# A new order for the first 330 of 1099 steps of a gated SSM-and-MLP kernel

## The chip, the cores and the metric

The kernel runs on one core of a Trainium2 chip. A core has five engines that each work through their own list of instructions: TensorE (PE, with its weight loads PEld), VectorE (DVE), ScalarE (ACT), GpSimd (POOL) and SyncE (SP), which here only issues DMAs. They meet at semaphores. The metric is the device time of one execution in microseconds.

## The reference

`S` is 2048, `D` 640, `F` 1536; all tensors are bfloat16. Two branches read the same `x` and are mixed by a gate per row.

```python
def _A_ref(q, k, v, shift_k, ssm_k, ssm_D):
    # k_shift: causal 4-tap filter of k along S, per column
    k_shift = sum(k_pad[:, t:t + S, :] * shift_k[:, ks - 1 - t] for t in range(ks))
    kv = k_shift * v
    # y: causal convolution of kv with ssm_k along S, by an FFT of length 2 S
    y = irfft(rfft(kv_pad) * rfft(ssm_k_pad))[:S] + kv * ssm_D
    return q * y

def _B_ref(x, w1, w2, w3, w4):
    h = _gelu(_layernorm(x) @ w1)
    # four column groups of h shifted by +1, -1, +2, -2 rows
    hs = concatenate([g0, g1, g2, g3]) @ w2
    x1 = x + hs
    return x1 + _gelu(_layernorm(x1) @ w3) @ w4

x = A_q
g = _sigmoid((x * gate_w).sum(-1, keepdims=True))
return g * _A_ref(x, A_k, ...) + (1 - g) * _B_ref(x, B_w1, ...)
```

(The sums and transforms are abridged here; `B_x` is not used.)

## The kernel before

Row `p * 16 + t` of a 2048 x 640 tensor lies in partition `p`, at place `t` of 16. Four places make a chunk, and there are four chunks, 0 to 3. The work is cut into 1099 numbered steps. The list `ORDER` names them in the order in which they are recorded; every engine gets its instructions in that order, and there is no scheduler behind it. A step `name.args:n` is the n-th part of a function, and letters such as `VAVA` in its name say which of its copies DVE (V) and ACT (A) make.

The first 330 steps hold, chunk by chunk:

- the loads of X (`load_x0` L193 in two halves for chunk 0, `load_x` L190), of k (`k_load:0` L563), of W1 in two halves (`load_w1` L197), of v in another row order by POOL's indirect DMA (`v_load` L173), and small ones (`load_cj` L542, `load_gw` L200, `d_fold:0` L401 and L402);
- row statistics (`x_stats`, DVE L685 to L695, ACT L679 and L681 for the rows given to it, the rstd on POOL L657 and L658) and the normalisation (`x_norm`, L662 on ACT, L664 on DVE);
- the transposition of the normalised chunk: for chunks 0 and 1 on PE (`x_turn`, L619, copied from PSUM at L360 by ACT or L362 by DVE), for chunks 2 and 3 by a DMA transpose that SP issues (L652);
- the W1 product (`mlp1:0`, five matmuls at L707 for each chunk and column group) and its GELU (`mlp1:1`, ACT L710);
- k's transposition on PE (L619 and L360 or L362 again), its wrap columns KW (`k_wrap`, L570 to L572), the tap diagonals DG (`kv_consts`, L552 and L553), and five `tap` steps, one for 128 columns each: 76 matmuls (L590) filter k, and DVE multiplies by v (L605 from PSUM, or L602 after an ACT copy at L599);
- the first transform stage (`step1`, pairs of matmuls at L423 and two copies each to a staging tile `stg`, stored to `S_x` by SP at L437 in two halves for each chunk);
- the loads of the filter (`load_h` L183 and L187) and its transposes on PE (`h_transpose` L390); the shifts of h on POOL (`h_shift` L742 to L761); the gate's rows and columns (`z_rows`, `z_cols`); the first W2 products (`w2`, L788, added to X by DVE at L791); sine tables by ACT (`f1_table`, `f4_table`, `t2_table`, L277).

Behind them come the rest of W2, the transform of the filter, the products and inverse transform, W3 (L840) and W4 (L867), and the output.

Two things tie the steps beside the order itself. PSUM has eight banks, handed out by the digits of `SLOTS["c"]` in the order of allocation. Tiles of one chunk (`kn`, `xn`, `stg` and others) share four row buffers, handed out by `SLOTS["row"]`; a tile that takes a buffer waits until the work on the one before it there has ended, a store included.

Of the kernel before, what the change touches and what calls it, by code (L numbers as in the profile page):

```python
# [41 lines left out]
def kernel(  # L42
# [24 lines left out]
        "c": "012345670124703510347205142356401723605162370514731057423671045261304732641374153670421350627413"  # L67
             "502634751264351270361427503164257364102546173045621537426107432715604371401362570164301257613045"
             "267236057416537621507362651374026372401534762501373150427102547535706432073125640736450750634127"
             "504763270415367204325170635147630125460327156034215760147362304167135620316425031672301402715320"  # L70
             "1724107361761423564023714053627501267420674256271306234",
        "row": "01230213021302320123012031203120310310303",
        "gt": "012301031010231012301201",
        "xt": "010101",
        "gq": "0120201201021020120122102121021021",
# [803 lines left out]
    def step4(t1, ev):  # L879
# [37 lines left out]
        "load_x0.1:0 "  # L917
        "consts0:1 "
        "warm:1 "
        "warm:2 "  # L920
        "pow0:0 "
        "kv_alloc:0 "
        "k_load.3.AVA:0 "
        "f4_table:0 "
        "x_stats.0.VVVA:0 "
        "warm:3 "
        "k_load.3.AVA:1 "
        "x_stats.0.VVVA:1 "
        "load_x.1:0 "
        "x_stats.0.VVVA:2 "  # L930
        "k_load.3.AVA:5 "
        "x_stats.0.VVVA:3 "
        "x_stats.0.VVVA:4 "
        "x_stats.0.VVVA:5 "
        "x_stats.0.VVVA:6 "
        "warm:4 "
        "row_order:0 "
        "k_load.2.VAV:0 "
        "f1_table:0 "
        "x_norm.0.VVAA:0 "  # L940
        "x_norm.0.VVAA:1 "
        "f4_table:1 "
        "x_stats.1.VVVV:0 "
        "k_load.3.AVA:2 "
        "load_x.3:0 "
        "x_norm.0.VVAA:2 "
        "x_stats.1.VVVV:1 "
        "k_load.3.AVA:3 "
        "x_turn.0.AAA:0 "
        "k_load.3.AVA:6 "  # L950
        "k_load.2.VAV:5 "
        "load_w1.1:0 "
        "x_norm.0.VVAA:3 "
        "k_load.2.VAV:1 "
        "x_stats.1.VVVV:2 "
        "x_turn.0.AAA:1 "
        "x_stats.1.VVVV:3 "
        "x_turn.0.AAA:2 "
        "x_stats.1.VVVV:4 "
        "load_w1.0:0 "  # L960
        "x_stats.1.VVVV:5 "
        "x_stats.3.VVAA:0 "
        "k_load.3.AVA:4 "
        "x_norm.1.VVVV:0 "
        "x_turn.0.AAA:4 "
        "k_load.2.VAV:3 "
        "x_turn.0.AAA:3 "
        "x_turn.0.AAA:5 "
        "x_stats.3.VVAA:1 "
        "x_norm.1.VVVV:1 "  # L970
        "x_norm.1.VVVV:2 "
        "v_load.2:0 "
        "k_load.0.AAV:0 "
        "f1_table:1 "
        "mlp1.0.2:0 "
        "mlp1.0.3:0 "
        "x_norm.1.VVVV:3 "
        "v_load.0:0 "
        "k_load.1.AVV:0 "
        "k_load.2.VAV:6 "  # L980
        "mlp1.0.0:0 "
        "load_x.2:0 "
        "x_stats.3.VVAA:2 "
        "x_turn.1.VVV:0 "
        "x_turn.1.VVV:4 "
        "mlp1.0.1:0 "
        "x_stats.3.VVAA:3 "
        "x_turn.1.VVV:1 "
        "k_load.2.VAV:4 "
        "x_stats.3.VVAA:4 "  # L990
        "x_stats.3.VVAA:5 "
        "k_load.0.AAV:3 "
        "x_turn.1.VVV:5 "
        "mlp1.0.3:1 "
        "x_stats.3.VVAA:6 "
        "x_turn.1.VVV:2 "
        "v_load.3:0 "
        "x_turn.1.VVV:3 "
        "k_load.1.AVV:3 "
        "w1_mixed:0 "  # L1000
        "v_load.1:0 "
        "mlp1.0.0:1 "
        "x_stats.2.VVAA:0 "
        "mlp1.0.2:1 "
        "k_load.0.AAV:1 "
        "mlp1.0.1:1 "
        "x_stats.3.VVAA:7 "
        "k_load.0.AAV:5 "
        "mlp1.1.2:0 "
        "x_norm.3.VVVV:0 "  # L1010
        "x_norm.3.VVVV:1 "
        "k_load.0.AAV:4 "
        "load_cj:0 "
        "k_load.0.AAV:2 "
        "mlp1.1.2:1 "
        "x_norm.3.VVVV:2 "
        "x_norm.3.VVVV:3 "
        "x_stats.2.VVAA:1 "
        "k_load.1.AVV:5 "
        "mlp1.0.4:0 "  # L1020
        "k_load.1.AVV:4 "
        "mlp1.0.4:1 "
        "k_load.1.AVV:1 "
        "d_fold:0 "
        "mlp1.1.4:0 "
        "x_turn.3.D:0 "
        "kv_consts:0 "
        "x_stats.2.VVAA:2 "
        "mlp1.1.0:0 "
        "k_load.2.VAV:2 "  # L1030
        "k_wrap:0 "
        "k_load.1.AVV:6 "
        "mlp1.1.4:1 "
        "k_load.0.AAV:6 "
        "x_stats.2.VVAA:3 "
        "t2_table:0 "
        "load_w2:0 "
        "mlp1.1.3:0 "
        "k_load.1.AVV:2 "
        "tap.3.VAVA:0 "  # L1040
        "mlp1.1.0:1 "
        "x_stats.2.VVAA:4 "
        "h_shift.1:0 "
        "mlp1.1.3:1 "
        "tap.4.VAAV:0 "
        "x_stats.2.VVAA:5 "
        "tap.3.VAVA:1 "
        "tap.3.VAVA:3 "
        "tap.3.VAVA:5 "
        "h_shift.0:0 "  # L1050
        "mlp1.1.1:0 "
        "tap.4.VAAV:7 "
        "x_stats.2.VVAA:6 "
        "tap.3.VAVA:4 "
        "tap.4.VAAV:1 "
        "load_h.2:0 "
        "tap.3.VAVA:7 "
        "z_cols:0 "
        "mlp1.1.1:1 "
        "load_gw:0 "  # L1060
        "tap.4.VAAV:5 "
        "tap.4.VAAV:3 "
        "mlp1.3.1:0 "
        "tap.3.VAVA:2 "
        "x_stats.2.VVAA:7 "
        "x_norm.2.AVVV:0 "
        "mlp1.3.1:1 "
        "mlp1.3.4:0 "
        "tap.4.VAAV:2 "
        "mlp1.3.0:0 "  # L1070
        "x_norm.2.AVVV:1 "
        "tap.4.VAAV:8 "
        "x_norm.2.AVVV:2 "
        "x_norm.2.AVVV:3 "
        "h_shift.0:1 "
        "tap.4.VAAV:6 "
        "tap.3.VAVA:6 "
        "mlp1.3.4:1 "
        "tap.4.VAAV:4 "
        "mlp1.3.0:1 "  # L1080
        "tap.2.AVAA:0 "
        "x_turn.2.D:0 "
        "h_shift.3:0 "
        "tap.0.AVAA:0 "
        "tap.2.AVAA:3 "
        "tap.2.AVAA:7 "
        "tap.2.AVAA:5 "
        "tap.3.VAVA:8 "
        "mlp1.3.3:0 "
        "tap.0.AVAA:3 "  # L1090
        "h_shift.0:2 "
        "tap.0.AVAA:5 "
        "tap.2.AVAA:8 "
        "h_shift.3:1 "
        "mlp1.3.2:0 "
        "tap.0.AVAA:4 "
        "tap.2.AVAA:6 "
        "tap.0.AVAA:1 "
        "mlp1.3.3:1 "
        "tap.0.AVAA:6 "  # L1100
        "tap.1.VAVA:0 "
        "tap.0.AVAA:7 "
        "tap.1.VAVA:5 "
        "tap.1.VAVA:1 "
        "tap.2.AVAA:4 "
        "mlp1.3.2:1 "
        "load_h.1:0 "
        "mlp1.2.2:0 "
        "tap.0.AVAA:8 "
        "tap.2.AVAA:1 "  # L1110
        "tap.1.VAVA:7 "
        "h_shift.1:1 "
        "tap.0.AVAA:2 "
        "load_h.3:0 "
        "mlp1.2.3:0 "
        "tap.1.VAVA:2 "
        "tap.1.VAVA:3 "
        "tap.2.AVAA:2 "
        "step1.KV.3.AAAVAVAAAV:9 "
        "tap.1.VAVA:8 "  # L1120
        "tap.1.VAVA:6 "
        "mlp1.2.2:1 "
        "mlp1.2.3:1 "
        "tap.1.VAVA:4 "
        "step1.KV.3.AAAVAVAAAV:11 "
        "step1.KV.3.AAAVAVAAAV:3 "
        "step1.KV.3.AAAVAVAAAV:10 "
        "step1.KV.3.AAAVAVAAAV:12 "
        "h_shift.0:3 "
        "step1.KV.3.AAAVAVAAAV:13 "  # L1130
        "step1.KV.3.AAAVAVAAAV:5 "
        "mlp1.2.4:0 "
        "step1.KV.3.AAAVAVAAAV:6 "
        "load_h.4:0 "
        "step1.KV.3.AAAVAVAAAV:0 "
        "step1.KV.3.AAAVAVAAAV:4 "
        "step1.KV.3.AAAVAVAAAV:14 "
        "h_shift.1:2 "
        "step1.KV.2.AVAVAVAAAA:6 "
        "z_rows:0 "  # L1140
        "z_rows:1 "
        "step1.KV.3.AAAVAVAAAV:2 "
        "step1.KV.3.AAAVAVAAAV:7 "
        "load_h.0:0 "
        "step1.KV.1.VAVAAAVVAA:0 "
        "step1.KV.3.AAAVAVAAAV:8 "
        "step1.KV.2.AVAVAVAAAA:8 "
        "step1.KV.3.AAAVAVAAAV:1 "
        "step1.KV.2.AVAVAVAAAA:3 "
        "z_rows:2 "  # L1150
        "mlp1.2.1:0 "
        "mlp1.2.1:1 "
        "h_shift.3:2 "
        "step1.KV.3.AAAVAVAAAV:16 "
        "step1.KV.1.VAVAAAVVAA:1 "
        "step1.KV.3.AAAVAVAAAV:15 "
        "mlp1.2.0:0 "
        "h_transpose.0.VV:2 "
        "step1.KV.2.AVAVAVAAAA:5 "
        "w2.0:0 "  # L1160
        "mlp1.2.4:1 "
# [903 lines left out]
```

## Time and profile before

| what | value |
|---|---|
| time, median of 3 runs | 231.19 us (227.55 to 232.08) |
| the profiled execution | 227.13 us, of which the span is 225.4 us |
| PE busy | 217.8 us, 97% of the span |
| DVE busy | 183.7 us, 81% |
| ACT busy | 171.4 us, 76% |
| granted TensorE clock | 1.0 |
| DMA moved | 57.61 MB |

The profile is one execution. A matmul's end is modelled, so a busy PE may still be slower than its best. In the timeline and the chain a row begins with its start and its length in us; a row of the timeline then has engine, line, operation, out<-in, the shape and the count, and in brackets how long the engine had sat idle and what ended that. In the chain each piece is what the next one waited for. In the table of waits the figures are the sum, the number of times and the longest.

### The profile page before, as it was taken

The page shows a single profiled execution, that of the slowest core. Times are in us where ns is not written, and L with a number is a line of the kernel's source. Part 1 is how long each engine was busy: PE and PEld are TensorE (multiplying, and loading weights), DVE is VectorE, ACT ScalarE, POOL GpSimd, SP SyncE. Part 2 cuts the span into 40 slices and gives each one's busy share as a digit, 9 for nine tenths or more (in the row PEclk, how much of TensorE's full clock was granted, in tenths as well). Part 3 has the DMA queues.
Part 4 walks back from the last instruction along what each step waited for, and adds up shares of the span by engine and source line. Part 5 has one row for each costly group of instructions (what it writes and reads, how often), then busy time and mean ns, then how long its engine had stood idle before and what let it go on. Part 6 is the DMA issues. An engine that isn't in the chain of part 4 may idle for free.

```text
span 225.4 us, 6053 instructions
## 1 busy us (share of the span) xinstructions
PE 217.8 (97%) x2427; PEld 121.5 (54%) x2428; DVE 183.7 (81%) x447; ACT 171.4 (76%) x341; POOL 38.1 (17%) x91
## 2 busy tenths in 40 slices
PE   8989999899999999999999999999999999999994
PEld 2557455447846563345664444556533547657762
DVE  7898998868889969963899988989999841439994
ACT  4899988787999999999987597967988450266450
POOL 4247246816000431300600000000000000000000
PEclk9999999999999999999999999999999999999999
DMA  6999998892998999999989570690794879429914
GB/s 226 374 376 344 258 280 170 317 364 107 361 365 355 348 295 265 410 334 343 254 219 338 116 243 0 191 379 17 119 305 166 249 259 366 175 60 305 324 70 179
DMA packets 41770, 57.61 MB, mean 256 GB/s; under 512 B 18446, under 2 KB 34446, under 8 KB 41486
## 3 DMA queue, kind: packets, MB, share of 16 engines
q1 hardware_dynamic: 41166, 54.60, 75.4%
q0 software_dynamic: 576, 2.62, 3.1%
q8 instruction: 19, 0.31, 0.6%
q14 instruction: 9, 0.07, 0.1%
HBM read 34.93 MB, written 18.35 MB: 236 GB/s over the span
## 4 chain that ended last, share of the span: by engine, by line
PE 79%; DMA 9%; DVE 4%; ACT 4%; issue 1%; POOL 1%; SPq 0%; ACTq 0%
PE ps L840 24%; PE ps L867 23%; PE psw L788 7%; PE ps L465 5%; PE ps L893 4%; DMA X<-in_A_q_dram 4%; PE psm L707 4%; DMA xt<-xn 3%; PE psz L228 3%; PE ps L512 3%; PE ps L423 2%; PE pst L390 2%; DVE X L791 2%; ACT stg L360 2%; DMA S_x<-stg 2%; PE psk L590 1%
## 5 line engine op out<-in xcount | busy, mean ns | idle before, releaser
L840 PE MATMUL ps<-x1t,W 128*128 128x512 bf16 x240 | 56.1, 380 | 0.1
L867 PE MATMUL ps<-W,gt 128*128 128x320 bf16 (+2 forms) x383 | 55.1, 299 | 0.1
L867 PEld LDWEIGHTS <-gt 128*128 128x128 bf16 x384 | 36.2, 98 | 17.7 <-issue 3.0
L844 ACT ACTIVATE gt<-ps 128x512 bf16<-128x512 f32 x48 | 27.6, 609 | 19.0 <-PE ps L867 10.6
L840 PEld LDWEIGHTS <-W 128*128 128x128 bf16 x240 | 21.9, 98 | 28.7 <-issue 5.9
L360 ACT CAST stg<-ps 128x512 bf16<-128x512 f32 x55 | 28.6, 604 | 2.3 <-PE ps L423 2.0
L870 DVE SCALAR_TENSOR_TENSOR X<-ps,OMG,X 128x320 bf16<-128x320 f32 (+2 forms) x32 | 17.2, 547 | 11.9 <-PE ps L867 11.7
L707 PE MATMUL psm<-xt,WA 128*128 128x512 bf16 x100 | 23.4, 379 | 1.9 <-DMA WA<-in_B_w_dram 0.8
L360 ACT CAST gs<-ps 128x320 bf16<-128x320 f32 x41 | 15.6, 440 | 8.8 <-PE ps L512 4.8
L788 PE MATMUL psw<-WA,HT 128*128 128x320 bf16 x116 | 21.4, 300 | 0.0
L362 DVE CAST XS<-ps 128x512 bf16<-128x512 f32 x19 | 12.5, 684 | 6.7 <-PE ps L465 6.7
L362 DVE CAST stg<-ps 128x512 bf16<-128x512 f32 x25 | 15.8, 683 | 1.9 <-PE ps L423 1.9
L707 PEld LDWEIGHTS <-WA 128*128 128x128 bf16 x100 | 9.2, 97 | 12.9 <-DMA WA<-in_B_w_dram 1.0
L360 ACT CAST hs<-ps 128x512 bf16<-128x512 f32 x28 | 15.0, 605 | 1.4 <-PE ps L465 1.4
L791 DVE SCALAR_TENSOR_TENSOR X<-psw,X 128x320 bf16<-128x320 f32 x32 | 14.5, 487 | 1.6 <-PE psw L788 1.6
L897 ACT ACTIVATE y<-ps,GS 128x320 bf16<-128x320 f32 x22 | 10.4, 526 | 5.7 <-PE ps L893 3.5
L710 ACT ACTIVATE HT<-psm 128x512 bf16<-128x512 f32 x20 | 11.8, 617 | 3.6 <-PE psm L707 3.5
L788 PEld LDWEIGHTS <-HT 128*128 128x128 bf16 x116 | 10.7, 98 | 6.8 <-issue 3.1
L362 DVE CAST gs<-ps 128x320 bf16<-128x320 f32 x23 | 10.7, 484 | 2.4 <-PE ps L512 1.7
L797 ACT ACTIVATE jk<-X 128x640 bf16<-128x640 bf16 x16 | 12.2, 761 | 0.5 <-DVE X L791 0.4
L788 PE MATMUL psw<-WA,HM 128*128 128x320 bf16 x44 | 12.3, 299 | 0.0
L360 ACT CAST XS<-ps 128x512 bf16<-128x512 f32 x21 | 11.8, 607 | 0.5 <-PE ps L465 0.3
(151 smaller groups left out, 346.6 us busy)
## 6 DMA issues: line engine op xcount, KB each, us to landing
S_x<-stg SPq DMA_DIRECT2D x8, 640.0 KB, 4.3
S_h<-stg SPq DMA_DIRECT2D x8, 640.0 KB, 4.8
ax<-S_x SPq DMA_DIRECT2D x8, 640.0 KB, 5.9
ax<-S_h SPq DMA_DIRECT2D x8, 640.0 KB, 8.1
S_g<-gs SPq DMA_DIRECT2D x8, 640.0 KB, 3.6
W<-in_B_w_dram SPq DMA_DIRECT2D x2, 1920.0 KB, 9.1
kn<-in_A_k_dram SPq DMA_DIRECT2D x4, 640.0 KB, 6.9
E<-in_A_ssm_k_dram SPq DMA_DIRECT2D x5, 512.0 KB, 6.1
```

Source lines behind the costliest of these rows:

```text
L360: A.copy(out=dst, in_=src)
L362: V.tensor_copy(out=dst, in_=src)
L465: PE.matmul(ps[j][q:q + 32, lo - 512 * u:hi - 512 * u], lhsT=CMP[HALF[j], 8 * b + 4 * h + i, c, :], rhs=st[name, 2 * b + h][HALF[j], i, lo ...
L707: PE.matmul(ps[:].rearrange("p (a b) -> p a b", a=4), lhsT=W1N[:, k, 160 * u:160 * u + P] if u < 4 else W1M[:, k, :], rhs=xt[:, :, k, :], ...
L710: A.activation(out=st["HT"][:, 4 * c:4 * c + 4, u, :], in_=ps[:].rearrange("p (t b) -> p t b", t=4), func=ACT.Gelu_apprx_tanh)
L788: PE.matmul(ps[:], lhsT=h_tile(f, t1), rhs=W2P[:, f, o:o + W], start=(f == 0), stop=(f == 4))
L791: V.scalar_tensor_tensor(out=X1[:, t1, o:o + W], in0=box["ps"][:], scalar=1.0, in1=X[:, t1, o:o + W], op0=ALU.mult, op1=ALU.add, accum_out ...
L797: A.activation(out=jk[:], in_=X1[:, t1, :], func=ACT.Square, accum_out=S12[:, 1, t1:t1 + 1])
L840: PE.matmul(ps[:].rearrange("p (a b) -> p a b", a=4), lhsT=st["W3"][:, k, f * P:(f + 1) * P], rhs=xt[:, :, k, :], start=(k == 0), stop=(k ...
L844: A.activation(out=st["gt", c, f // 4][:, f % 4, :], in_=ps[:], func=ACT.Gelu_apprx_tanh)
L867: PE.matmul(ps[:], lhsT=st["gt", c, f // 4][:, f % 4, i * P:(i + 1) * P], rhs=st["W4"][:, f, o:o + w], start=(f == 0), stop=(f == FC - 1))
L870: V.scalar_tensor_tensor(out=X1[:, t1, o:o + w], in0=box["ps"][:], scalar=OMG[:, t1:t1 + 1], in1=X1[:, t1, o:o + w], op0=ALU.mult, op1=ALU ...
```

## The change

The first 330 entries of `ORDER` are put in another sequence, and the letters of 21 of their functions change, so that some copies move between DVE and ACT. The last 769 entries are the same. `SLOTS` is renumbered to fit. No function changes, and every instruction that was there is there, but for one load of ACT's function tables, which the new order does not need.

```diff
-        "row": "01230213021302320123012031203120310310303",
+        "row": "01230120132030201320132103210321031031010",
...
-        "open.L1.left:0 "
-        "open.A2.right:0 "
-        "consts0:0 "
-        "load_x0.0:0 "
-        "warm:0 "
...
+        "open.L1.left:0 open.A2.right:0 warm:0 warm:1 warm:2 warm:3 warm:4 load_x0.0:0 consts0:0 consts0:1 "
```

On SP, at the program's start, the loads stood like this before (X is `A_q`, kn a chunk of k, WA with `B_w` first W1 and further down W2, E the filter, cr the taps, dr ssm_D, GW the gate weights):

```order
L193 DMA X<-in_A_q_dram 128x1280 x2
L563 DMA kn<-in_A_k_dram 128x2560
L190 DMA X<-in_A_q_dram 128x2560
L563 DMA kn<-in_A_k_dram 128x2560
L190 DMA X<-in_A_q_dram 128x2560
L197 DMA WA<-in_B_w_dram 128x5x320 x2
L563 DMA kn<-in_A_k_dram 128x2560 x2
L190 DMA X<-in_A_q_dram 128x2560
L542 DMA cr<-in_A_shift_k_dram 128x5x4
L401 DMA dr<-in_A_ssm_D_dram 1x3x128
L402 DMA dr<-in_A_ssm_D_dram 1x2x128
L652 DMA_TRANSPOSE xt_504<-xn 128x20x128
```

and now:

```order
L193 DMA X<-in_A_q_dram 128x1280 x2
L190 DMA X<-in_A_q_dram 128x2560
L563 DMA kn<-in_A_k_dram 128x2560
L190 DMA X<-in_A_q_dram 128x2560
L563 DMA kn<-in_A_k_dram 128x2560
L197 DMA WA<-in_B_w_dram 128x5x320 x2
L563 DMA kn<-in_A_k_dram 128x2560 x2
L542 DMA cr<-in_A_shift_k_dram 128x5x4
L200 DMA GW<-in_gate_w_dram 128x5x1
L190 DMA X<-in_A_q_dram 128x2560
L652 DMA_TRANSPOSE xt_777<-xn 128x20x128
L183 DMA E<-in_A_ssm_k_dram 128x2048
```

X and k have changed places among the first four chunk loads: X came in the chunk order 1, 3, 2 behind chunk 0 and comes as 3, 1, 2; k came as 3, 2, 0, 1 and comes as 2, 3, 1, 0. The last chunk of X stands behind the taps and the gate weights. The transpose shown is that of chunk 3.

On DVE, ahead of that transpose, this stood before (b and the L686 rows are statistics, the last L664 row is the normalisation of chunk 3, xt the transposed chunk 1):

```order
L362 COPY xt<-pst 128x1024
L203 COPY WA<-WA 128x640
L685 BN_STATS b_433<-X 128x6 x2
L686 BN_AGGR mv<-b_433 128x2
L664 TENSOR_SCALAR xn<-X,RS,NB 128x640 x4
L362 COPY KT<-pst 128x1024
L552 TENSOR_REDUCE i_507<-IDB 128x32
L553 TENSOR_TENSOR DG<-i_507,cr 128x640
```

and now, where the first L664 row is chunk 1 and the second chunk 3:

```order
L664 TENSOR_SCALAR xn<-X,RS,NB 128x640 x4
L570 MEMSET KW 128x15
L571 COPY KW<-KT 128x15x64
L572 COPY KW<-KT 128x15x63
L362 COPY KT<-pst 128x1024 x2
L552 TENSOR_REDUCE i_460<-IDB 128x32
L553 TENSOR_TENSOR DG<-i_460,cr 128x640
L362 COPY xt<-pst 128x1024
L362 COPY xt<-pst 128x512
L664 TENSOR_SCALAR xn<-X,RS,NB 128x640 x4
L685 BN_STATS b_660<-X 128x6 x2
L686 BN_AGGR mv<-b_660 128x2
```

The wrap columns and the diagonals have moved ahead of chunk 3's normalisation, and chunk 2's statistics behind it.

On ACT, around the copy of the gate rows (zr), the new order is this, where HT is a GELU of `mlp1`, the two stg rows ahead of zr belong to chunk 1 of the first transform and the stg rows behind it to chunk 2:

```order
L360 CAST stg<-ps_1136 128x512
L360 CAST stg<-ps_1130 128x512
L723 COPY zr<-psz 128x512
L360 CAST stg<-ps_1181 128x512
L710 ACTIVATE HT<-psm_1189 128x4x128
L360 CAST stg<-ps_1185 128x512
L360 CAST stg<-ps_1179 128x512
L710 ACTIVATE HT<-psm_1210 128x4x128
```

Chunk 1 now goes through the first transform together with chunk 3, ahead of chunk 2; before, chunks 1 and 2 both followed chunk 3, mixed with each other. By `SLOTS["row"]` the row behind zr takes the buffer of chunk 3's upper half, and the second stg row behind it that of chunk 1's upper half.

More of the change, by code (lines that the diff above doesn't have):

```diff
@@ L933 @@
[L933 to L990, printed above, removed]
@@ L1011 @@
[L1011 to L1072, printed above, removed]
@@ L1073 @@
[L1073 to L1132, printed above, removed]
@@ L1269 @@
-        "step1.HT0.2.VAVAAAAAAA:6 "
-        "load_w3:0 "
-        "w2.6:0 "
-        "step1.HT0.2.VAVAAAAAAA:2 "
-        "i_tables:1 "
-        "step1.HT0.2.VAVAAAAAAA:7 "
-        "w2.10:0 "
-        "w2.2:2 "
-        "w2.5:1 "
-        "step1.HT0.2.VAVAAAAAAA:11 "
-        "d_fold:1 "
-        "step1.HT0.2.VAVAAAAAAA:8 "
-        "w2.8:0 "
-        "step1.KV.0.VAAVAAAAAV:15 "
-        "w2.1:4 "
-        "w2.6:1 "
-        "w2.8:1 "
-        "w2.12:0 "
-        "step1.HT0.2.VAVAAAAAAA:10 "
@@ L1560 @@
-        "x1_norm.2.AVVV:5 "
-        "w3.1.2:1 "
-        "product.1:3 "
-        "product.1:4 "
-        "product.6:0 "
-        "step3.7.AAAAAVAV:6 "
-        "w4.0:3 "
-        "w3.1.9:1 "
-        "step2.h.0.AAVAAAAAVA:4 "
-        "step3.7.AAAAAVAV:9 "
-        "gather.h.2:0 "
-        "step3.7.AAAAAVAV:7 "
-        "product.6:1 "
-        "w3.1.1:0 "
-        "step3.1.VAAVVVAA:5 "
-        "step3.1.VAAVVVAA:7 "
-        "x1_norm.3.AVAA:1 "
-        "w3.1.8:0 "
-        "x1_norm.3.AVAA:2 "
@@ L2008 @@
-        "store.8:1 "
-        "close.L2:0 "
-        "close.C:0 "
[169 rows of a table added]
     ).split()
```

887 lines of the change are left out of this document (7 added, 880 removed), and 168 rows, old and new, of the table ORDER.

## The prediction

> **What bounds the kernel now.** I read the page's busy shares first, then busy time by stretch, then the chain of waits, then the timeline of the first 60 us.
>
> ```profile
> PE 217.8 (97%) x2427; PEld 121.5 (54%) x2428; DVE 183.7 (81%) x447; ACT 171.4 (76%) x341; POOL 38.1 (17%) x91
> ```
>
> In the table by stretch, the columns are the stretch, its length, busy us of PE, PEld, DVE, ACT and POOL, the clock, the DMA share and GB/s.
>
> ```profile
> 32.00:65.10 33.10, 32.24 (x467) 19.51 (x467) 27.42 (x63) 28.42 (x51) 14.85 (x34) 1.00 0.81 274
> 65.10:88.90 23.80, 23.66 (x165) 13.04 (x162) 21.04 (x75) 22.44 (x48) 4.81 (x11) 1.00 1.01 327
> 88.90:225.40 136.50, 133.02 (x1454) 72.35 (x1454) 106.41 (x201) 93.57 (x196) 5.90 (x18) 1.00 0.71 226
> ```
>
> From 65.1 us on PE is full. The 3.5 us that it lacks in the last row lie nearly all behind its last matmuls, which end at 221.3 by the chain:
>
> ```profile
> 219.00 2.34 PE ps L867 x10
> ```
>
> The 769 steps that stay as they are begin, on PE, with the third pair in this row of PE's timeline (64.65, 64.88, 65.09):
>
> ```profile
> 64.65 0.82 PE L423 MATMUL ps<-KV,F 64*128 64x512 bf16 x6
> ```
>
> So the change is worth what it moves that moment, 65.09 us: behind it nothing can take up a delay and nothing can lose a gain. The reordered part, by the chain:
>
> ```profile
> 8.96 1.01 ACT KT L360
> 9.97 0.82 ACT xn L662
> ...
> 12.09 0.91 ACT xt L360
> ...
> 13.42 8.33 DMA X<-in_A_q_dram
> ...
> 21.78 0.90 DVE b L685 x2
> ...
> 23.14 1.15 DVE xn L664 x3
> ...
> 24.32 7.63 DMA xt<-xn
> ...
> 32.00 3.41 PE psm L707 x15
> 35.41 2.00 PE psk L590 x151
> ...
> 40.83 0.59 ACT yk L599
> ...
> 44.31 3.59 ACT stg L360 x7
> ...
> 47.91 4.30 DMA S_x<-stg
> ```
>
> Chunk 2 of X lands at 21.75; the statistics of chunk 2 stand in DVE's order ahead of the normalisation of chunk 3; that ends at 24.3, its DMA transpose lands at 31.95, and PE starts the W1 products of chunk 3 at 32.00. PE's own waits up to 65.1 us are few; the four largest (sum, times, longest):
>
> ```profile
> PE psz L228 <- DVE NPI L248: 1.0, 1, 1.0
> PE psm L707 <- DMA WA<-in_B_w_dram: 0.8, 1, 0.8
> PE psm L707 <- ACT yk L599: 0.8, 1, 0.8
> PE pst L619 <- DMA kn<-in_A_k_dram: 0.7, 1, 0.7
> ```
>
> They sum to 3.3 us. The first is the start itself, so an order without any wait would save little over 2.3 us, or 1.0%.
>
> **The start.** The transfers land by their place in SP's queue: the third at 8.3, the fourth at 9.85, the fifth at 11.4, W1 at 14.2.
>
> ```profile
> 4.36 0.74 ACT L679 ACTIVATE jk<-X 128x640 bf16<-128x640 bf16 x1 [2.36 <-DMA X<-in_A_q_dram]
> 5.22 0.74 ACT L681 ACTIVATE jk<-X 128x640 bf16<-128x640 bf16 x1
> 6.07 1.28 ACT L277 ACT_TABLE_LOAD   x1
> 7.14 0.16 DVE L695 TENSOR_SCALAR VE<-mv 128x3 f32<-128x3 f32 x1
> 8.29 0.86 PE L619 MATMUL pst<-IDB,kn 128*128 128x128 bf16 x12
> 9.85 0.89 DVE L685 BATCH_NORM_STATS2 b<-X 128x6 f32<-128x320 bf16 x2 [0.32 <-DMA X<-in_A_q_dram]
> 11.43 0.86 PE L619 MATMUL pst<-IDB,kn 128*128 128x128 bf16 x12 [0.71 <-DMA kn<-in_A_k_dram]
> 14.22 3.41 PE L707 MATMUL psm<-xt,WA 128*128 128x512 bf16 x15 [0.82 <-DMA WA<-in_B_w_dram]
> ```
>
> W1 keeps its place, sixth and seventh, in both orders; "ahead of two k chunks" was so before, and I cost it at nothing. The third is now chunk 3 of X. ACT takes three statistics passes of it before it normalises chunk 0, at 0.86 each (4.36 to 5.22): 8.3 + 2.6 = 10.9. Then come two normalisations (0.82), one k copy (1.01 with its latency, 0.9 at pace), and the small and the large copy of the transposed chunk 0 (0.5 and 0.9): 10.9 + 1.6 + 0.9 + 1.4 = 14.8. The W1 products start there instead of at 14.2, 0.6 late. The table load at 6.07 is gone, since the order needs four loads and not five; ACT waited for data there anyway (2.36 idle), so it is worth nothing. F4's table leaves DVE's start, whose time goes into waiting for X. On the PE the five warm-up steps now run in one piece; they end before the fourth transfer at 9.85, which holds the first k chunk.
>
> **DVE up to chunk 3's transpose.** Here lies the term that counts. The normalisation of chunk 3 no longer waits for chunk 2 of X; behind it go 0.9 of chunk 2's statistics (21.78 row) and 0.9 of F4's small operations. But ahead of it now stand the wrap columns KW and the diagonals DG, and copies of k trade places with ACT:
>
> ```profile
> 24.82 0.36 DVE L552 TENSOR_REDUCE i<-IDB 128x32 bf16<-128x128 bf16 x1
> 25.21 0.83 DVE L553 TENSOR_TENSOR DG<-i,cr 128x640 bf16<-128x640 bf16 x1
> 25.95 0.68 DVE L362 COPY KT<-pst 128x1024 bf16<-128x1024 bf16 x1
> 26.57 0.41 DVE L571 COPY KW<-KT 128x960 bf16<-128x960 bf16 x1
> 26.89 0.80 DVE L572 COPY KW<-KT 128x945 bf16<-128x945 bf16 x1
> ```
>
> DG is 1.2, KW 1.1 (26.57 to 27.69), two k copies 1.2 at a pace of 0.6: 3.5 in. Going out are the 1.8 named and two small shares that went to ACT (0.4). Net +1.3. Idle time grows too: about 1.2 until chunk 3 lands at 8.3 (the statistics of chunk 0, which end at 7.3 today, end near 7.0 without F4) and 0.4 until the fifth transfer, against the 0.8 that DVE waits for X today: with 0.2 for ACT's late last sum, +0.7 to +1.0. I take +1.95 in all: the transpose is issued at 24.3 + 1.95 = 26.25. It lands 6.6 to 7.6 us later if it behaves as the two in this stage did; I take their median (the last figure of a row):
>
> ```profile
> 19.85 0.94 POOL L173 DMA_INDIRECT KV<-in_A_v_dram,ROWS  x1 [0.30 <-issue]
> ...
> KV<-in_A_v_dram,ROWS POOLq DMA_INDIRECT x4, 7.8
> x1t<-xn SPq DMA_TRANSPOSE x4, 5.1
> xt<-xn SPq DMA_TRANSPOSE x2, 7.1
> ```
>
> 26.25 + 7.1 = 33.35. What PE does before chunk 3 is the same amount as today: nine W1 steps and three tap steps in place of ten and two (1.1 against 1.0 each, the 32.00 and 35.41 rows), so without waits it would be ready at about 32.1. It waits 1.25, and starts chunk 3 at 33.35 instead of 32.00: **+1.35**. Today's 0.8 wait for the yk copy comes from a W1 product right behind the last tap step, which now has copies before it: **-0.75**.
>
> Queues passed: on SP the gate weights and cr now stand ahead of chunk 2 of X, which DVE reaches only at 26.3, so it has time. On POOL the last v chunk, issued at 19.85 today, moves behind chunk 3's rstd, 1.3 later; with 7.8 to land it is there at 28.9, and DVE's first tap product, which waits for all four, is due at 28.6: 0.3 that only DVE pays. d_fold's loads and the gate columns move to places where PE and DVE have other work; the columns cost the same matmuls wherever they are.
>
> **The stores.** A chunk of the first transform needs two of four row buffers. Chunks 3 and 1 now take all four, so the first ACT copy and the first DVE copy of chunk 2 wait for the store of chunk 3's upper half. From 33.35, PE has eight W1 steps (8.8), two tap steps (2.0) and seven pairs (1.7) until chunk 3 is through, and ACT three copies (0.5 each): stored at 47.4, landed 4.3 later at 51.7. ACT stands there from 49.4: it waits 2.3, and behind it queue the GELU of the next W1 products and the copies that free PE's banks. DVE waits 0.6, and later about 1.6 for chunk 2's own store, before it empties chunk 0. PE has eight banks to fill meanwhile. The cost for PE is between 0 and those 2.3 + 1.6. Today's like wait (47.91 to 52.21) cost PE almost nothing, as this row shows, so I take **+0.3**.
>
> ```profile
> 50.00:55.00 5.00, 4.90 (x48) 3.62 (x46) 3.79 (x9) 4.79 (x11) 3.59 (x6) 1.00 0.20 80
> ```
>
> Sum: 1.35 - 0.75 + 0.3 = +0.9 us. The profiled execution took 227.13 us (225.4 of span and 1.7 around it), so it would be 228.0.
>
> **The rivals.** *The transpose is quick.* The later four took 5.1, not 7.1: landed at 31.35, no wait on PE, and then 32.1 - 32.0 - 0.75, about -0.65: 226.5. For it: with the four X and k loads over by then, less lies beside it. Against it: the v chunk and W2 still do. The Trainium skill's "DMA: Bandwidth & Descriptors", section "Latency and other measured facts", gives a DMA transpose 261 GB/s or more; 655 KB would then be an estimated 2.5 us, landing at 28.8. The 7.1 row is far under that rate, so the trace so far disagrees; by that rule too PE would not wait, and the time is the same 226.5, from the rows as above.
>
> *The stores bind.* ACT's 2.3 and DVE's 1.6 fall on PE whole, because the eight banks hold nothing but results those two have yet to copy: 1.35 - 0.75 + 3.9 = +4.5, 231.6. It decides at the second pair of chunk 2: if a bank for it comes free only after 51.7, PE stands. Against it: two of the steps in between need banks that DVE frees.
>
> *It nets out.* The waits change places and the moment 65.09 does not move: 227.1. It lies inside my own sum's error, and I count it with the forecast.
>
> **How the numbers follow.** The forecast, +0.9 with 0 to +2.5 around it, 54%; the quick transpose 24%, and 5% more by the skill's rule; the stores 14%; 3% for what I do not see. The four executions known took 227.13, 227.55, 231.19 and 232.08 us: they differ by more than any term here, and the shown median, 231.19, is 1.8% over the profiled one. I put the 0.9 on the middle of the four, (227.55 + 231.19) / 2 = 229.4: 230.3. The range goes from 227.13 - 1.3 = 225.8 (a quick transpose with a little more, on a fast execution) to 232.1 + 1.5 = 233.6; the stores on a fast execution, 231.6, are inside. Two per cent, 4.6 us, is about what this kernel's measurement can tell from no change. A gain of that size would need more than all of PE's waits; I leave 6% for it. The stores reach it at their full price only: with what I do not see, 11% for slower. 83% for no difference.
>
> **What would show it.** Right: the first W1 product of chunk 3 near 33.3 with PE waiting for the transpose, the first at 14.8, the third tail pair near 66, and PE full from there on. The DVE step is wrong if the transpose is issued before 25.5; the landing is wrong if it takes under 6 us; the stores are wrong if PE shows waits for ACT or DVE copies between 49 and 61 of over 1 us. The whole is wrong if PE, behind 66 us, shows waits that it does not have today.

## The result, and the profile after

The changed kernel takes 228.96 us (median of 20 runs), the kernel before 227.67 (median of 20). The ratio is 1.0058, with a 95% interval of 1.0037 to 1.0078: slower by 0.6%, 1.3 us. A second timing of the same pair gave 1.0067 (1.0030 to 1.0105). The median of 231.19 shown before the change came from three runs, two of them long ones.

The page's first part of the kernel after, and its busy time by stretch (the stretch, its length, busy us of PE, PEld, DVE, ACT and POOL, the clock, the DMA share, GB/s), cut at the places that answer to those of before:

```profile
PE 218.4 (96%) x2428; PEld 121.4 (53%) x2428; DVE 184.3 (81%) x448; ACT 169.5 (74%) x336; POOL 38.0 (17%) x91
```

```profile
33.16:66.53 33.37, 32.59 (x405) 18.81 (x396) 29.73 (x85) 26.91 (x48) 15.72 (x34) 1.00 0.86 286
66.53:88.57 22.04, 21.65 (x157) 12.41 (x154) 19.25 (x68) 20.52 (x44) 4.18 (x8) 1.00 1.02 306
88.57:227.90 139.33, 134.91 (x1464) 72.88 (x1463) 108.37 (x208) 95.51 (x199) 6.53 (x21) 1.00 0.72 227
```

The kept 769 steps begin on PE with the third pair of this row of its timeline, at 66.52. (Ten of these 769 names carry the changed letters; behind the tail pair DVE and ACT still have the same instructions in both kernels.)

```profile
66.08 0.82 PE L423 MATMUL ps<-KV,F 64*128 64x512 bf16 x6
```

One trace each would mislead here, so I took two more of both kernels. The third tail pair stands at 65.09, 64.73 and 64.66 in the kernel before and at 66.52, 65.30 and 66.44 in the kernel after. The means, 64.83 and 66.09, differ by 1.26 us, close to the 1.3 that the times show, though the three traces of the kernel after lie 1.2 us apart. The start makes most of that spread. PE's first W1 product comes at 14.22, 13.81 and 13.79 in the kernel before and at 14.82, 13.38 and 14.54 in the kernel after, and from there to the tail pair it is 50.9 us in all three traces of the one and 51.7, 51.9 and 51.9 in those of the other. So 0.95 of the 1.26 lies behind the start and is there in every trace; 0.3 lies in the start, and that part is uncertain. PE's waits up to there (sum, times, longest), kernel after, first trace:

```profile
PE psk L590 <- DVE KV L605: 1.1, 3, 0.4
PE pst L619 <- DMA kn<-in_A_k_dram: 1.1, 2, 0.9
PE psz L228 <- DVE NPI L248: 1.0, 1, 1.0
PE psm L707 <- DMA xt<-xn: 0.5, 1, 0.5
PE pst L619 <- ACT xn L662: 0.3, 1, 0.3
PE psm L707 <- ACT xt L360: 0.2, 1, 0.2
```

The first row is new, and in all three traces (1.1, 1.1, 1.0); the row for k is in two of them. The new one is at the tap step ahead of chunk 3. This is PE's timeline there, and under it DVE's and POOL's:

```profile
28.11 2.33 PE L707 MATMUL psm<-xt,WA 128*128 128x512 bf16 x10
30.37 0.23 PE L590 MATMUL psk<-DG,KT 32*128 32x128 bf16 x1
30.97 0.21 PE L590 MATMUL psk<-DG,KT 32*128 32x128 bf16 x1 [0.37 <-DVE KV L605]
31.57 0.21 PE L590 MATMUL psk<-DG,KT 32*128 32x128 bf16 x1 [0.39 <-DVE KV L605]
32.16 0.38 PE L590 MATMUL psk<-DG,KT 32*128 32x128 bf16 x13 [0.39 <-DVE KV L605]
...
33.16 3.41 PE L707 MATMUL psm<-xt,WA 128*128 128x512 bf16 x15
```

```profile
27.68 0.21 DVE L686 BATCH_NORM_AGGREGATE mv<-b 128x2 f32<-128x12 f32 x1
30.22 2.49 DVE L605 TENSOR_TENSOR KV<-psk,KV 128x512 bf16<-128x512 f32 x4 [2.33 <-DMA KV<-in_A_v_dram,ROWS]
```

```profile
16.88 1.01 POOL L657 TENSOR_TENSOR RS<-VE,EXPO 128x4 f32<-128x4 f32 x1 [7.83 <-DVE VE L695]
...
18.34 1.22 POOL L173 DMA_INDIRECT KV<-in_A_v_dram,ROWS  x1 [0.18 <-issue]
...
23.67 1.02 POOL L173 DMA_INDIRECT KV<-in_A_v_dram,ROWS  x1 [0.16 <-issue]
```

Read from the bottom: POOL idles 7.83 us until chunk 1's statistics are done, and all four gathers of v stand behind that rstd. The first is issued at 18.34, where it was 15.84 before; the packets of the last one end at 29.30. DVE is ready for its first tap product at 27.9 and stands 2.33 us for that gather (2.1 to 2.3 in the three traces). Four products that read PSUM (L605) come at once then, and PE's third tap step, which needs the four banks that they free, takes 30.37 to 33.16: 2.8 us instead of 1.1 (2.8 and 2.6 in the other two traces). The order before reaches its first tap product three us after its last gather's packets have ended (27.66):

```profile
30.98 0.42 DVE L602 TENSOR_TENSOR KV<-yk,KV 128x512 bf16<-128x512 bf16 x1
```

The loss goes on behind chunk 3's first products. The next two tap steps take 2.4 to 2.5 us in the three traces of the kernel after and 1.9 to 2.0 in those of the kernel before; in the middle of them PE pauses for 0.2 to 0.3 us, for nothing that the view names:

```profile
37.51 0.75 PE L590 MATMUL psk<-DG,KT 32*128 32x128 bf16 x45 [0.23 <-issue]
```

Against these losses stand two waits of the kernel before: one of 0.2 to 0.5 for a GELU, which is gone, and one of 0.8 to 1.1 ahead of chunk 2's products, of which 0.4 to 0.8 is left.

Chunk 3's transpose was issued at 25.89 and landed 6.7 later, at 32.6, half a us ahead of the product that needs it. Nothing waited for it.

Behind the tail pair the first two traces seemed to say more: PE ends 156.9 us after it in the kernel before and 158.0 in the kernel after, with two waits that were not there before (kernel after, PE, from 66 us on):

```profile
PE ps L867 <- DMA W<-in_B_w_dram: 1.0, 1, 1.0
PE psw L788 <- ACT stg L360: 0.4, 1, 0.4
```

The third trace of the kernel *before* shows the same two:

```profile
PE ps L867 <- DMA W<-in_B_w_dram: 0.9, 1, 0.9
PE psw L788 <- ACT stg L360: 0.4, 1, 0.4
```

They come with a slower first transpose of X1 on SP (start, length of its issue), here in the kernel before, first and third trace:

```profile
78.09 4.40 SPq L821 DMA_TRANSPOSE x1t<-xn  x1
```

```profile
77.66 5.69 SPq L821 DMA_TRANSPOSE x1t<-xn  x1
```

So they do not need the new order. Whether it makes them more frequent stays open: that transpose pauses, by 0.15 to 1.95 us, in all eight traces of the new order and its variants, and in three of the six of the old order and its variants. In the six traces of the two kernels themselves PE ends 2.2 us later on the mean, 1.26 of it at the tail pair and 0.9 behind. The times, 1.3 us and 1.5 in the second timing, have room for only a part of that 0.9.

### The profile page after: what moved, and what is told of

Its sections match the earlier page's. It is cut to its first block, busy times and chain, and to the rows that moved or that the text cites. A ratio compares the mean times of both kernels' runs of the same rounds, so it can differ in the third digit from the quotient of the medians.

```text
span 227.9 us, 6050 instructions
## 1 busy us (share of the span) xinstructions
PE 218.4 (96%) x2428; PEld 121.4 (53%) x2428; DVE 184.3 (81%) x448; ACT 169.5 (74%) x336; POOL 38.0 (17%) x91
## 4 chain that ended last, share of the span: by engine, by line
PE 73%; DMA 14%; DVE 6%; POOL 3%; issue 1%; SPq 1%; DVEq 0%; POOLq 0%
PE ps L867 23%; PE ps L840 20%; PE psw L788 8%; DMA W<-in_B_w_dram 5%; PE psm L707 4%; DMA X<-in_A_q_dram 4%; PE ps L893 4%; PE ps L465 4%; PE ps L423 4%; PE ps L512 3%; DMA KV<-in_A_v_dram,ROWS 3%; DMA xt<-xn 3%; PE pst L390 2%; DVE b L685 1%; POOL KV L173 1%; DVE X L791 1%
## 5 line engine op out<-in xcount | busy, mean ns | idle before, releaser
L360 ACT CAST stg<-ps 128x512 bf16<-128x512 f32 x51 | 27.1, 600 | 5.1 <-DMA S_x<-stg 2.0
L707 PE MATMUL psm<-xt,WA 128*128 128x512 bf16 x100 | 23.8, 380 | 0.8 <-DMA xt<-xn 0.5
L362 DVE CAST stg<-ps 128x512 bf16<-128x512 f32 x29 | 18.4, 683 | 2.7 <-DMA S_x<-stg 1.6
L707 PEld LDWEIGHTS <-WA 128*128 128x128 bf16 x100 | 8.9, 97 | 11.9 <-issue 2.0
```

The lines of the kernel that those rows point to most:

```text
L360: A.copy(out=dst, in_=src)
L362: V.tensor_copy(out=dst, in_=src)
L707: PE.matmul(ps[:].rearrange("p (a b) -> p a b", a=4), lhsT=W1N[:, k, 160 * u:160 * u + P] if u < 4 else W1M[:, k, :], rhs=xt[:, :, k, :], ...
```

## The experiments

All of them compute the whole reference. An experiment is the named kernel with rows of `ORDER` moved; `SLOTS` stays as it was, except in the last one. Ratios are to the kernel before.

### The last gather ahead of the rstd

```diff
+"v_load.3:0 "
 "x_stats.3.VVAA:7 "
...
-"v_load.3:0 "
```

> The kernel after, with one row moved on POOL: the gather of the last v chunk (v_load.3) stands ahead of chunk 3's rstd again, as it did before the change. In the kernel after, it is issued at 23.67, lands at 30.1, and DVE waits 2.3 us for it ahead of its first tap product; the third tap step on PE (30.37) then takes 2.86 us instead of 1.1. The prediction's step (the gather is late because it was put behind that rstd, which takes 1.3 on POOL): it lands 1.3 earlier, at about 28.8, the third tap step loses some 1.3 us less, and the first chunk-3 W1 product is left to its transpose, which goes from 32.6 to about 33.5, because the rstd that the normalisation needs is now 1.0 later. Rival (the four gathers move one after the other, from 20.3 to 29.3, about 2.2 us each, so that the place of the last one's issue does not matter as long as it is ahead of 26.6): it lands at 29.8 to 30.1 as now, DVE waits as now, chunk 3 starts at 33.2 to 33.5, and the third tail pair stands at 66.5 to 67.0; time against the kernel after +0.0 to +0.4 us.

Measured: 1.0078 (1.0049 to 1.0108), no better than the kernel after. The gather did come earlier, its packets ending at 27.60 against 28.22 to 29.30. But the 1.0 to 1.3 us of the rstd that it passed went to the other side, as DVE's waits show:

```profile
DVE xn L664 <- POOL NB L658: 0.7, 1, 0.7
DVE KV L605 <- DMA KV<-in_A_v_dram,ROWS: 0.5, 1, 0.5
```

DVE now waits for chunk 3's rstd and reaches the taps later. PE's third tap step did shrink, to 1.7 us (29.46 to 31.16), but PE lost that elsewhere: it waits 1.1 us for chunk 2's transpose and 2.4 for k. The tail pair stood at 65.41; the trace of the unchanged kernel that starts much alike (13.38, here 13.10) has 65.30. Both expectations missed in part: mine on the landing, which did move, the other on the gain, which did not come. In this place of POOL's queue a change of places is a trade.

### The first gather ahead of chunk 1's rstd

```diff
+"v_load.2:0 "
 "x_stats.1.VVVV:5 "
...
-"v_load.2:0 "
```

> The kernel after, with one row moved on POOL: the first gather of v (v_load.2) ahead of chunk 1's rstd, where POOL is idle from 9.05 to 16.88. It is issued near 9.1 and moves beside the k chunks, chunk 1 of X and W1. If the run of four gathers sets the first tap products (mine now): three gathers are left from 18.3 on, the last lands near 27.7 instead of 30.1, DVE no longer waits 2.3, the third tap step takes about 1.1 to 1.4 instead of 2.86, and the first chunk-3 W1 product comes at 32.6, held by its transpose (issued 25.89, landing 6.7 later); DVE is then earlier by up to 2 us when it normalises chunk 2, so that the wait of 0.54 for that chunk's transpose at 43.5 goes too. Third tail pair at 65.3 to 65.6 instead of 66.52, time about 1 us below the kernel after, level with the kernel before. If the prediction's step holds (chunk 3's transpose alone sets PE, the gathers cost DVE 0.3): no more than 0.5 us. If the early gather pushes W1 and the k chunks back by its 1.7 us of the DMA engines: first W1 product at 15.5 to 16.5 instead of 14.82, and nothing gained.

Measured: 1.0015 (0.9980 to 1.0050). Of the 1.3 us, 1.0 is back. The intervals of this run and of the kernel after still touch (1.0050 and 1.0037), but the two later builds that keep this move came out level as well, at 1.0018 and 1.0010. The trace, DVE and then PE:

```profile
28.49 2.48 DVE L605 TENSOR_TENSOR KV<-psk,KV 128x512 bf16<-128x512 f32 x4 [0.37 <-PE psk L590]
```

```profile
30.60 0.40 PE L590 MATMUL psk<-DG,KT 32*128 32x128 bf16 x16
30.83 0.27 PE L590 MATMUL psk<-DG,KW 32*128 32x32 bf16 x12
30.93 0.76 PE L590 MATMUL psk<-DG,KT 32*128 32x128 bf16 x48
31.62 3.41 PE L707 MATMUL psm<-xt,WA 128*128 128x512 bf16 x15
...
41.61 1.25 PE L707 MATMUL psm<-xt,WA 128*128 128x512 bf16 x5 [0.65 <-DMA xt<-xn]
```

DVE no longer waits for v. The third tap step takes 1.1, the next two take 1.9, chunk 3 starts at 31.62 without a wait, and the tail pair stands at 64.67. The wait for chunk 2's transpose, which I expected to go, stayed. W1 was not pushed back (13.14); the k chunks were, and PE waits 3.3 us for them in place of 1.1.

### An earlier start

```diff
-"x_stats.3.VVAA:4 "
...
 "x_turn.0.VAA:3 "
+"x_stats.3.VVAA:4 "
```

> The kernel after, with one step moved on ACT: the third statistics pass of chunk 3 (two passes of one column make one step of 0.86) behind the copies of the transposed chunk 0, so that ACT normalises chunk 0 one pass earlier. By the prediction's start term (0.6 late because of these passes): the first W1 product comes at 14.0 instead of 14.82. If the start reaches the end, the third tail pair comes at 65.7 to 65.9 instead of 66.52. If the gathers of v set the tap steps (landing at 30.1, whatever PE did ahead of them): the third tap step loses as much more as PE has gained, chunk 3 starts at 33.2 as now, the third tail pair stays at 66.3 to 66.6, and the time does not move.

Measured: 1.0078 (1.0043 to 1.0114): nothing gained. The first W1 product came at 13.08 and the tail pair at 65.31, earlier than either branch had them. But the trace of the unchanged kernel that starts at 13.38 has its tail pair at 65.30, so this start gave nothing beyond what a good landing of the loads gives. Its 0.3 us were lost ahead of the tap steps already, where PE waits for chunk 1's normalisation (0.7 us here, 0.2 there). The third tap step then took 2.5 us, as late gathers make it:

```profile
PE pst L619 <- DVE xn L664: 0.7, 1, 0.7
```

```profile
29.31 0.50 PE L590 MATMUL psk<-DG,KT 32*128 32x128 bf16 x2
30.20 0.21 PE L590 MATMUL psk<-DG,KT 32*128 32x128 bf16 x1 [0.39 <-DVE KV L605]
30.80 0.38 PE L590 MATMUL psk<-DG,KT 32*128 32x128 bf16 x13 [0.39 <-DVE KV L605]
```

Both moves together:

> The kernel after with both moves at once: the first gather of v ahead of chunk 1's rstd (alone it took back about 1.0 of the 1.3 us), and the third statistics pass of chunk 3 behind chunk 0's copies on ACT (alone it gave nothing). If the gathers hid the gain of the earlier start, the two together give more than the first alone: first W1 product at 13.0 and the third tail pair at 64.0 to 64.5 against 64.67, time 0.3 to 0.6 us under the first alone, level with the kernel before or 0.3 under it. If PE is held by the k chunks at 17 to 20 us (waits of 0.64 and 1.00 in the run with the first move alone), the start gives nothing again: third tail pair at 64.6 to 64.9, ratio to the kernel before 1.000 to 1.003.

Measured: 1.0018 (0.9976 to 1.0060), the same as the gather alone. The second branch holds in its ratio, not in its tail pair. The trace (first W1 product at 13.93, tail pair at 65.83) drew slow k loads, with 3.0 us of waits for them, DVE waits 1.3 us for the last gather again, and no gain from the start shows either.

### Late gathers in the kernel before

```diff
-"v_load.2:0 "
...
-"v_load.0:0 "
...
-"v_load.3:0 "
...
-"v_load.1:0 "
...
 "x_stats.3.VVAA:7 "
+"v_load.2:0 v_load.0:0 v_load.3:0 v_load.1:0 "
```

> The kernel before, with one thing made late: all four gathers of v behind chunk 3's rstd on POOL, so that the first is issued near 20.8 instead of 15.84, five us later. If the gathers set the first tap products: the four move from about 22.8 to 31.6 at 2.2 each, the last lands near 32.3, DVE's first tap product (30.98 in the kernel before) comes at 32.3, and the tap steps ahead of it stand for banks: the third tail pair goes from 65.09 to 66 to 67.5, time +1 to +2.5 us against the kernel before. By the prediction's step (a late gather is paid by DVE only): DVE waits 1.3, PE nothing, and the third tail pair stays within 0.3 of 65.09. Chunk 3's own rstd comes up to 1.4 earlier, which gives nothing, since its normalisation waits on DVE behind chunk 2's statistics.

Measured: 1.0711 (1.0625 to 1.0797), 17 us in four runs, where I had expected 1 to 2.5. It is another mechanism than either theory had. SP's queue, and PE:

```profile
23.56 9.92 SPq L652 DMA_TRANSPOSE xt<-xn  x1
```

```profile
30.42 1.24 PE L707 MATMUL psm<-xt,WA 128*128 128x512 bf16 x5
47.06 3.17 PE L707 MATMUL psm<-xt,WA 128*128 128x512 bf16 x7 [15.40 <-DMA xt<-xn]
```

Chunk 3's transpose was issued between the second and the third gather. Its issue alone took 9.92 us instead of 3.8 to 4.1, it landed 23.5 us later, and the gathers' last packet ended at 46.2. To see which of the two slows the other, I let the transpose wait until the gathers are in:

```diff
-"x_norm.3.VVVV:3 "
-"x_turn.3.D:0 "
...
 "tap.3.VAVA:4 "
+"x_norm.3.VVVV:3 "
+"x_turn.3.D:0 "
```

> The kernel before with late gathers (the run before_v_late, where chunk 3's transpose was issued at 23.6 in the middle of them and landed 23.5 us later, at 47.1, and the gathers themselves ended at 46.2), and with the last normalisation of chunk 3 behind DVE's first tap product, which waits for the gathers: the transpose is issued only when they have landed, W2's load ahead of it. If the transpose and the gathers slow each other (mine): the four gathers run from 23.7 to about 31 to 33, the transpose is issued at 32 to 35 and lands 5 to 6.5 later, at 37 to 41, so that issued ten us later it lands six to ten us earlier; the time is 237 to 241 instead of 245.4. If the gathers alone are slow so late in the program, or the transpose is slow by itself at that place: gathers until 40 or later, transpose at 50 or later, time 248 or more.

Measured: 1.0429 (1.0366 to 1.0493), 237.04 us against 245.35. The gathers, left alone, ended at 32.1, fourteen us earlier; the transpose was issued at 33.92, ten us later, and landed at 38.9, eight us earlier:

```profile
33.92 3.30 SPq L652 DMA_TRANSPOSE xt<-xn  x1
```

```profile
38.91 3.53 PE L707 MATMUL psm<-xt,WA 128*128 128x512 bf16 x8 [7.97 <-DMA xt<-xn]
```

They slow each other. (W2's load ran beside both from 33.5 us on in the slow run, but by then the transpose's issue had already taken its 9.92 us.)

### The early gather in the kernel before

The same move of `v_load.2` as above, in the kernel before.

> The kernel before with the first gather of v ahead of chunk 1's rstd, where its POOL is idle from 8.95 to 14.38; the same move as the one that took back 1.0 us from the kernel after. In the kernel before the first tap product is due on DVE at 30.98 and the gathers have ended by 27.7, so that nothing waits for them: if only a wait for the gathers is worth something, the time stays within 0.1 per cent. Where the gathers end earlier, the transpose of chunk 3 has less beside it (6.1 to 7.6 now, 4.9 to 5.0 where they end within 2 us of its issue): it lands at 29 to 30, which removes the wait of 0.2 at 32.0 and no more, 0.1 to 0.2 us. If the early gather delays W1 and the k chunks here, where PE already waits 0.7 and 0.8 for them, it costs up to 1 us.

Measured: 1.0091 (1.0049 to 1.0134), 2 us slower. The last branch has the sign, but not the size or the place. The gather moved beside the loads, and the last chunk of X came later. DVE's order before has its statistics ahead of chunk 3's normalisation:

```profile
23.38 0.89 DVE L685 BATCH_NORM_STATS2 b<-X 128x6 f32<-128x320 bf16 x2 [2.34 <-DMA X<-in_A_q_dram]
...
24.43 1.48 DVE L664 TENSOR_SCALAR xn<-X,RS,NB 128x640 bf16<-128x640 bf16 x4
```

Chunk 3's transpose was issued at 25.93 instead of 23.6 to 24.3, and the tail pair stood at 67.24. The new order has no such place, since it takes chunk 2's statistics behind that normalisation; so the move that helps one order hurts the other.

### More traces of both kernels

> The kernel after, unchanged, for a second trace: how far two executions of one kernel differ at the places of the argument. In the first trace the first W1 product came at 14.82 and chunk 1's rstd began at 16.88; in three variants that leave the start alone, or move one step of it, the product came at 13.1 and the rstd at 15.4. If the first trace drew a slow landing of the k chunk (11.37 to 12.83 for the same packets), this one shows 13.1 and 15.4, the gathers of v end near 28 instead of 29.3, DVE waits under 1.5 us for them instead of 2.3, and the third tail pair stands at 65.2 to 65.8. If the change sets it, it shows 14.8, 16.9 and 66.5 again. The wait for W4 (1.0 at 107.5) is, by the variants (0.15 to 1.5 with W4 issued 29.7 behind the tail pair each time), a spread of the landing, and lies between 0 and 1.6.

> The kernel before, unchanged, for a second trace. Third tail pair at 64.8 to 65.4 (65.09 in the first), chunk 3's transpose issued at 24.3 and landed 6 to 8 later beside the last gathers, and a wait for W4 between 0 and 1.6 where the first trace had none: if it is over 0.5, the 1.0 that the kernel after showed there is no part of the difference between the kernels.

> The kernel before against itself, with a third trace. In the two traces of it PE waits nowhere behind the third tail pair and ends 156.9 us after it; in two traces of the kernel after and in six variants PE ends 157.2 to 158.6 after it, with a wait of 0.2 to 1.5 for W4, behind a transpose of X1 that pauses 0.2 to 2.0 at 16.4 to 17.1 us past the tail pair. If the pause is chance, this third trace shows one as likely as not (end at 157.2 or more); if it belongs to the changed order, it shows none again, and 156.9. The ratio to itself should hold 1.000 in its interval, and the interval says what five rounds can tell.

> The kernel after once more, with a third trace and its own five rounds: ratio to the kernel before 1.004 to 1.008 if the 1.0058 of the first timing stands. Third tail pair at 65.2 to 66.6; DVE waits 2.0 to 2.3 for the last gather, as in both traces of it, and PE's third tap step takes 2.8 us; the end comes 157.6 to 158.6 after the tail pair if the pause behind it belongs to the changed order, and 156.9 in some traces if it is chance.

Measured: the kernel after took 229.05 us in one run beside 228.04 for the kernel before, and the timing of it is the 1.0067 given above; the kernel before against itself 1.0003 (0.9966 to 1.0040). The tail pairs are in the result. The first W1 product of the kernel after comes at 14.82, 13.38 and 14.54: how the first loads land moves the start by more than the 0.6 that I had argued about. DVE's wait for the last gather does not depend on that (2.3, 2.3, 2.1), since a start that is earlier for DVE is earlier for the gathers too. I had expected under 1.5 there if the start was slow by chance, and that was wrong. The two waits behind the tail pair come and go in one and the same kernel: the second trace of the kernel before showed none, the third both.

### A version to beat both

Some fifty of the first 340 steps moved by a few places, the early gather among them (the expectation says some twenty), and 17 digits of `SLOTS` with them; one copy of the first transform (not two, as the expectation has it) goes to ACT. The two that stand for the rest, the second as SP sees it:

```diff
-"x_norm.1.VVVV:1 "
+"x_norm.1.VAVV:1 "
...
-"load_x0.1:0 load_x.3:0 k_load.2.AVA:0 "
+"k_load.2.AVA:0 load_x0.1:0 load_x.3:0 "
```

> The kernel after with the first gather of v ahead of chunk 1's rstd (which alone came level with the kernel before, 1.0015), and some twenty steps of the first 340 moved by a few places, digits of PSUM banks with them: one normalisation of chunk 1 on ACT instead of DVE, so that DVE normalises chunk 3 about 1 us earlier; the tap products that free PSUM banks ahead of others; two copies of the first transform on ACT. If DVE's order ahead of the two transposes is what is left (a wait of 0.65 for chunk 2's transpose and 1.6 for the k chunks in the run with the first move alone): chunk 3's transpose issued at 25.3 to 25.6 instead of 26.1, chunk 2's at 34.6 to 34.9 instead of 35.5, third tail pair at 63.8 to 64.5 instead of 64.67, ratio to the kernel before 0.996 to 1.000. If the k chunks hold PE at 17 to 20 us whatever DVE does, or the earlier transpose meets the last gathers and lands later, as much later as it is issued earlier: third tail pair at 64.6 to 65.5, ratio 1.001 to 1.004.

Measured: 1.0010 (0.9983 to 1.0036). Level with the kernel before, not faster. PE waits less on the whole, but the k chunk that I let pass two loads of X on SP put the start off:

```profile
PE pst L619 <- DVE xn L664: 1.2, 1, 1.2
PE psz L228 <- DVE NPI L248: 1.0, 1, 1.0
PE ps L423 <- DVE KV L602: 0.6, 1, 0.6
PE pst L619 <- ACT xn L662: 0.5, 1, 0.5
```

The first W1 product comes at 15.42, two us later than with the early gather alone, and the transposes are issued at 26.3 and 36.3, no earlier, and the tail pair stands at 66.10, later than either branch had it. In this timing the kernel before took 229.06 us itself, so that 66.10 can't be set beside the other traces. No run here beat the kernel before.

## Why the prediction was right or wrong

**The frame held in the main.** The change was worth about what it moved the tail pair: 1.26 us in the traces, 1.3 in the times. I had +0.9. "PE full from there on" did not hold: all three traces of the kernel after show waits behind 66 us, which I had named as a sign that the whole is wrong. The third trace of the kernel before has such waits too, and the times leave room for only a part of them; how much of the 1.3 they make stays open.

**The number failed at its base.** The step was "I put the 0.9 on the middle of the four": 229.4, against a median of 227.67 in 20 runs. On the profiled execution the sum gave 228.0. By that choice the forecast of 230.3 lay under the shown median of 231.19, and so told of a kernel that is not slower, while its own working said slower by 0.4%. The sentence beside it, that about 2% is what can be told from no change, was wrong as well. It took the spread of single runs for the uncertainty of a median: 20 runs tell 0.2%, and the 0.6% is well outside that.

**The term of +1.35 had the wrong cause, and was too large.** Chunk 3's first product came at 33.16, 31.69 and 32.68, against 32.00, 31.48 and 31.46 before: +0.86 on the mean. The issue of the transpose, 26.25 by the sum, came 0.4 to 1.9 early (25.89, 24.40, 25.65), and 24.40 is under the 25.5 that I had named as the sign of a wrong DVE step. The landing 7.1 later was near (6.7, 6.6, 6.2). PE's wait of 1.25 for it failed: no trace of the kernel after has a wait there. PE came later than the transpose, by another road. The step that failed is "On POOL the last v chunk [...] moves behind chunk 3's rstd, 1.3 later; with 7.8 to land it is there at 28.9, [...] 0.3 that only DVE pays". It counted the queue that this one gather passed, and not what stands ahead of all four: chunk 1's rstd. It comes 1.0 to 2.6 us later (15.33 to 16.88 against 14.23 to 14.38), because chunk 1 of X is the fifth transfer and no longer the fourth (DVE waits 0.6 and 0.3 us for it in two traces of three), and DVE takes two of chunk 3's four places ahead of it. The landing was 30.1 and DVE's wait 2.3. That only DVE pays failed too, because the products behind that wait free the banks of PE's next tap step. The early gather gave 1.0 of the 1.3 back; an early start, and the last gather's place, gave nothing.

**The term of -0.75 was half there as a wait, and gave nothing.** I took the row "psm L707 <- ACT yk L599: 0.8" for a wait that the new order removes. In the two other traces of the kernel before the same product waits 1.1 and 1.0 us, and the row names the transpose of chunk 2:

```profile
PE psm L707 <- DMA xt<-xn: 1.1, 1, 1.1
```

Two releasers came within 0.1 us of each other, and the view names the last. With the yk copy out of the way the wait for chunk 2's transpose stays, 0.4 to 0.8 in the kernel after: 0.4 less on the mean of three. The tap steps behind chunk 3 lose 0.5 again. From chunk 3's first product to the tail pair the kernel after takes 33.4, 33.6 and 33.8 us and the kernel before 33.1, 33.2 and 33.2, so this stretch came out at +0.4 where the sum had -0.75 + 0.3.

**The start.** 14.8 was predicted for the first W1 product and the first trace had 14.82, but the mean of three is 14.25, against 13.94 before. The 0.6 is 0.3, and taking an ACT pass off its path gave nothing at the end.

**The stores.** ACT and DVE wait for row buffers as worked out, 2.3 and 2.2 predicted (first rows: ACT, DVE in the kernel after, 20 to 62 us):

```profile
ACT stg L360 <- DMA S_x<-stg: 2.0, 1, 2.0
```

```profile
DVE stg L362 <- DMA S_x<-stg: 1.6, 2, 1.0
```

PE shows no wait between 49 and 61 in any of the three traces, so the term is 0 and not +0.3, and the rival in which the stores bind is out.

**The quick transpose** is out in the form that I gave it, 5.1 beside the gathers. With the gathers ended within 2 us of its issue it lands in 4.9 to 5.0 (last section), and then PE does not wait for it, as that rival had it. By the rate that the Trainium skill's "DMA: Bandwidth & Descriptors" gives in its section "Latency and other measured facts", 261 GB/s, it would take an estimated 2.5 us. The measured time decides: chunk 3's transpose takes no less than 4.9 us in any run here, which is 134 GB/s, even with the gathers over.

## What to carry to other kernels

A moved load has to be followed through every queue behind it: here a chunk of X one place later held an rstd, the rstd held POOL, POOL's queue held four gathers, and their landing held PSUM banks. Where a wait's releaser has a neighbour within 0.1 us, removing the one that the view names removes next to nothing; a second trace may name the other. And for effects under 1%, the base is the median of many runs, and the sum's own sign has to survive the choice of the base.

## What the runs showed of the hardware

A DMA transpose and POOL's gathers slow each other. The records of chunk 3's transpose (640 KB), by how long the last gather's packets ran on behind its issue:

| kernel | transpose issued | last gather packet ends | landed after |
|---|---|---|---|
| before, gathers late, transpose later | 33.92 | 32.13 | 4.9 |
| after, first gather early | 26.11 | 26.58 | 5.0 |
| tuned | 26.28 | 27.02 | 5.0 |
| after, last gather earlier | 25.76 | 27.60 | 4.9 |
| after, both moves | 26.65 | 29.26 | 5.8 |
| before, third trace | 23.59 | 26.47 | 5.7 |
| before, second trace | 23.65 | 26.85 | 6.1 |
| after, third trace | 25.65 | 29.10 | 6.2 |
| after, first trace | 25.89 | 29.30 | 6.7 |
| before, first trace | 24.32 | 27.66 | 7.6 |
| after, earlier start | 24.85 | 28.35 | 6.2 |
| after, second trace | 24.40 | 28.23 | 6.6 |
| before, gathers late | 23.56 | 46.21 | 23.5 |

(The early gather in the kernel before is left out, since its trace has no landing for this transpose.) Up to 2 us of overlap cost nothing, 2.6 to 3.8 us went with 0.8 to 2.7 more, and the transpose issued before the third gather took 18.6 more, with its 256-byte packets at 62 ns each on the mean instead of 21 to 29 in the thirteen other traces. Only the two runs with late gathers were made to test this; in the others more than the gathers differs. What the engines do in that case the records do not tell; it stays open.

The gather issued at 9.55, when SP's loads were under way, moved its first packet at 14.41, while one issued at 16.84 moved its first at 19.82: the early place on POOL was not an equally early transfer. And the first transpose of X1 pauses by 0 to 2 us, 16.4 to 17.1 us behind the tail pair, in executions of the same program. The wait for W4 that follows (0 to 1.5 us) is the largest chance term seen here, and its cause is not settled.
